# Token chunks of two fused feed-forward layers: six pairs of 512 to 488 columns in place of five of 512 and one of 448

## Chip, cores and metric

The kernel runs on one core of a Trainium2 chip. The metric is the device time of one execution in microseconds (us), from three executions of the kernel before: 1044.4, 1044.48 and 1044.66, so the median is 1044.48 us.

## What is computed

The input is a matrix v of 256 channels by N = 6016 tokens. An attention over channels mixes its rows, and two feed-forward layers of inner width 2048 follow, all in 32-bit floating point.

```python
qn = q / (np.linalg.norm(q, axis=1, keepdims=True) + 1e-06)
kn = k / (np.linalg.norm(k, axis=1, keepdims=True) + 1e-06)
s = kn.transpose(0, 2, 1) @ qn / tau          # 256 x 256
a = softmax(s, axis=-1)
x = (v @ a).reshape(6016, 256)
h = x @ w_in;  x = (h / (1 + np.exp(-1.702 * h))) @ w_out           # layer 0
h = x @ w_in2; x = (np.maximum(h, 0) + alpha * np.minimum(h, 0)) @ w_out2   # layer 1
```

## The kernel before, in words

A first stage (about 52 us) computes the 256 x 256 matrix of scores, its softmax, and folds it into the first layer's inner weights. What is left is two layers over the tokens, and these take nearly all the time.

**Tiling.** The tokens stand along the free axis, cut into 12 chunks whose widths are the list WIDTHS (L28). Two neighbouring chunks make a pair, so there are six pairs per layer, numbered 0 to 5. Within a pair both chunks have the same width n. Each layer's 2048 inner units are cut into eight groups (index j) of two blocks of 128.

**Precision.** Every operand is kept as a high and a low half of type fp32r. A product is three matmuls with 128 x 128 weights and n moving columns each (PASSES, L37): high by high, high weights by low data, and low weights by high data. Each matmul has its own weight load.

**A quartet** (L766 to L846) is the work of one j of one pair: four blocks of the hidden layer (two blocks of units by two chunks) from seven products instead of eight, after Strassen and Winograd. The operands T1 to T4 of the seven products are sums and differences of the pair's blocks of data (prepare, L527). That makes 7 x 3 = 21 inner matmuls (L651, into the PSUM tile ps_h). Between them stand the outer products of the quartet before (Outs.next, L666 to L683): eight of three matmuls each, 24 in all (L680, into ps_o). So TensorE issues 45 matmuls in a quartet, eight quartets in a pair, 360 in a pair. Pair 0 of layer 0 is computed without that trick (direct, L744) with 24 inner and 24 outer matmuls for each j, always 512 columns wide (T). Layer 0 has quartets for its pairs 1 to 5 and layer 1 for its pairs 0 to 5: eleven pairs of quartets.

**Other engines.** ScalarE copies some of the PSUM tiles to SBUF (L777), applies the activation (L722, L726) and makes the high half (L734, L736). VectorE adds the two parts of a block (L711), does the second step of layer 1's activation (L730) and makes the low half (L740, L742). Beside these it runs steps from a list in the background: operands of the next pair (L541 to L550) and conversions of weights. That list is a planner's: each step has a fixed cost (0.7 us and so on), and a step is taken where the cost fits into a fixed gap (FREE, L31). Neither depends on the width.

**Transfers.** The chunks of the next pair are loaded at the second quartet of a pair (load_tokens, L245, called at L959 and L960), on SyncE's queue. A pair's results are copied from PSUM at its end (evacuate, L687 to L696) and stored: in layer 0 to the buffer x1 in device memory, in layer 1 to the output. The buffer x1 has a separate tensor for each chunk, with rows of n elements.

**Memory.** All SBUF and PSUM tiles of tokens are 512 columns wide whatever n is, and only their first n columns are used. The operands T3, T4 and B22 of the even pairs of layer 1 come from a separate pool (xin2, L537); all others come from one ring of eleven tiles.

**Order.** The order of the instructions on every engine is written out by hand (manual_schedule) and does not depend on the widths.

```python
WIDTHS = [512] * 10 + [448] * 2                                    # L28
...
n = WIDTHS[c0]                                                     # L769
...
nc.tensor.matmul(ps[:, :n], WI[:, wq, a, blk], x[:, b, :n], ...)   # L651
...
nc.tensor.matmul(acc_ps[c][d][:, :n], WO[:, j, a, f, d * P:(d + 1) * P], (hi, lo)[b][:, :n], ...)   # L680
```

Of the kernel before, what the change touches and what calls it, by code (L numbers as in the profile page):

```python
# [24 lines left out]
SLOTS = 4  # L25
RAWS = 2

WIDTHS = [512] * 10 + [448] * 2  # L28
assert sum(WIDTHS) == N

FREE = ((0.7, 2.8, 1.7), (0.0, 0.8, 0.8))  # L31
# [24 lines left out]
def attention_then_two_ffns(ctx: ExitStack, tc: tile.TileContext, q, k, vT, tau, w1i, w1o, w2i, w2o, alpha, outT):  # L56
# [14 lines left out]
    nc = tc.nc  # L71
    starts = [sum(WIDTHS[:c]) for c in range(len(WIDTHS))]
    NP = len(WIDTHS) // 2

# [12 lines left out]
    WO = wto.tile([P, NQ, 2, 2, C], F32R, name="wo")  # L87
    x1 = [dram.tile([P, 2, w], F32, name=f"x1_{c}") for c, w in enumerate(WIDTHS)]
    w2i_d = [dram.tile([P, 2, 7, P], F32R, name=f"w2i_{j}") for j in range(NQ)]
# [155 lines left out]
    def load_tokens(l, c):  # L245
        n = WIDTHS[c]
        raws[l, c] = cv.tile([P, 2, T], F32, tag="xraw", name="xraw", bufs=2)
        src = x1[c][:] if l else vT[:, starts[c]:starts[c] + n].rearrange("(a p) n -> p a n", p=P)
        nc.sync.dma_start(raws[l, c][:, :, :n], src)

    with tc.manual_schedule():
# [275 lines left out]
        def prepare(l, p):  # L527

            n = WIDTHS[2 * p]
            r0, r1 = raws.pop((l, 2 * p)), raws.pop((l, 2 * p + 1))  # L530
# [513 lines left out]
```

## Time and profile before

| what | value |
|---|---|
| median of three executions | 1044.48 us |
| the profiled execution, its own time | 1045.86 us |
| its span, from the first to the last instruction | 1044.1 us |
| TensorE clock granted, mean | 1.000 |
| TensorE busy (matmuls) | 1034.2 us, 99% of the span, 4658 matmuls |
| TensorE weight loads busy | 865.6 us, 83% |
| VectorE busy | 815.0 us, 78% |
| ScalarE busy | 750.6 us, 72% |
| mean traffic with device memory | 74 GB/s |

Matmuls overlap: the next one starts before the one ahead of it has left the array. So the busy share of TensorE is no measure of its speed, and neither is the duration of one matmul. What counts is the distance from the start of one matmul to the start of the next, which the timeline and the lengths of stages give. Below it is called the pace.

### The profile page before, as it was taken

The page shows a single profiled execution, that of the slowest core. Times are in us where ns is not written, and L with a number is a line of the kernel's source. Part 1 is how long each engine was busy: PE and PEld are TensorE (multiplying, and loading weights), DVE is VectorE, ACT ScalarE, POOL GpSimd, SP SyncE. Part 2 cuts the span into 40 slices and gives each one's busy share as a digit, 9 for nine tenths or more (in the row PEclk, how much of TensorE's full clock was granted, in tenths as well). Part 3 has the DMA queues.
Part 4 walks back from the last instruction along what each step waited for, and adds up shares of the span by engine and source line. Part 5 has one row for each costly group of instructions (what it writes and reads, how often), then busy time and mean ns, then how long its engine had stood idle before and what let it go on. Part 6 is the DMA issues. An engine that isn't in the chain of part 4 may idle for free.

```text
span 1044.1 us, 12624 instructions
## 1 busy us (share of the span) xinstructions
PE 1034.2 (99%) x4658; PEld 865.6 (83%) x4658; DVE 815.0 (78%) x1318; ACT 750.6 (72%) x1255; POOL 32.6 (3%) x43
## 2 busy tenths in 40 slices
PE   8999999999999999999999999999999999999998
PEld 7788888888888888888998888888888888888897
DVE  5789978888788888555647888888888888888776
ACT  6677668777687777667767777777777777767775
POOL 4400000000000000000110000000000000000000
PEclk9999999999999999999999999999999999999999
DMA  9625203115225223003444002002001000100100
GB/s 359 235 75 174 74 11 106 61 56 177 76 81 177 76 96 131 1 1 122 161 167 152 1 1 82 1 1 81 1 1 47 35 1 21 57 1 1 41 1 35
DMA packets 30462, 77.63 MB, mean 74 GB/s; under 512 B 3008, under 2 KB 7616, under 8 KB 30144
## 3 DMA queue, kind: packets, MB, share of 16 engines
q1 hardware_dynamic: 28096, 65.29, 17.6%
q0 software_dynamic: 2304, 11.54, 3.3%
q8 instruction: 36, 0.59, 0.3%
q14 instruction: 26, 0.21, 0.1%
HBM read 52.96 MB, written 23.86 MB: 74 GB/s over the span
## 4 chain that ended last, share of the span: by engine, by line
PE 89%; DMA 4%; ACT 3%; DVE 3%; issue 1%; SPq 0%; ACTq 0%; DVEq 0%
PE ps_o L680 47%; PE ps_h L651 41%; DMA qk<-in_q 2%; ACT ghi L736 1%; PE pw L474 1%; ACT g L722 1%; DMA qs<-in_q 1%; DMA xraw<-in_vT 1%; DVE g L711 1%; DMA qk<-in_k 0%; ACT s L777 0%; DVE glo L742 0%; PE gram L337 0%; DVE ob L694 0%; DVE top L133 0%
## 5 line engine op out<-in xcount | busy, mean ns | idle before, releaser
L680 PE MATMUL ps_o<-ghi,wo 128*128 128x512 f32 (+1 forms) x1536 | 563.7, 386 | 0.0
L651 PE MATMUL ps_h<-x,wi 128*128 128x512 f32 (+1 forms) x2040 | 554.5, 387 | 1.0 <-ACT wi L482 0.7
L651 PEld LDWEIGHTS ps_h<-x,wi 128*128 128x128 f32 x2040 | 381.1, 188 | 78.4 <-ACT s L777 3.2
L680 PEld LDWEIGHTS ps_o<-ghi,wo 128*128 128x128 f32 x1536 | 288.3, 188 | 55.5
L680 PE MATMUL ps_o<-glo,wo 128*128 128x512 f32 (+1 forms) x768 | 296.2, 386 | 0.5 <-DVE glo L740 0.5
L711 DVE TENSOR_TENSOR g<-ps_h,s 128x512 f32<-128x512 f32 (+1 forms) x264 | 178.5, 676 | 92.5 <-PE ps_h L651 53.8
L777 ACT COPY s<-ps_h 128x512 f32<-128x512 f32 (+1 forms) x264 | 152.1, 576 | 91.3 <-PE ps_h L651 90.1
L734 ACT ACTIVATE ghi<-g,sign_sb 128x512 fp32r<-128x512 f32 (+1 forms) x192 | 136.8, 713 | 71.6 <-DVE g L730 70.1
L740 DVE SCALAR_TENSOR_TENSOR glo<-g,sign_sb,ghi 128x512 fp32r<-128x512 f32 (+1 forms) x192 | 141.3, 736 | 44.7 <-ACT ghi L734 38.4
L680 PEld LDWEIGHTS ps_o<-glo,wo 128*128 128x128 f32 x768 | 144.2, 188 | 28.5 <-DVE glo L740 0.8
L742 DVE TENSOR_TENSOR glo<-g,ghi 128x512 fp32r<-128x512 f32 (+1 forms) x192 | 126.0, 674 | 32.9 <-ACT ghi L736 32.9
L726 ACT ACTIVATE g<-g,sign_sb 128x512 f32<-128x512 f32 (+1 forms) x144 | 102.3, 711 | 28.2 <-DVE g L711 28.2
L730 DVE SCALAR_TENSOR_TENSOR g<-g,slope_sb 128x512 f32<-128x512 f32 (+1 forms) x144 | 105.8, 735 | 18.9 <-ACT g L726 18.8
L736 ACT CAST ghi<-g 128x512 fp32r<-128x512 f32 (+1 forms) x192 | 113.2, 611 | 3.6
L722 ACT ACTIVATE g<-g 128x512 f32<-128x512 f32 (+1 forms) x120 | 74.7, 623 | 38.0 <-DVE g L711 37.8
L722 ACT ACTIVATE g<-ps_h 128x512 f32<-128x512 f32 (+1 forms) x72 | 42.1, 585 | 10.4 <-PE ps_h L651 9.6
L337 PE MATMUL gram<-qk 128*128 128x256 f32 x156 | 33.9, 379 | 1.9 <-DMA qk<-in_k 1.9
L730 DVE SCALAR_TENSOR_TENSOR g<-ps_h,slope_sb,g 128x512 f32<-128x512 f32 (+1 forms) x48 | 35.0, 730 | 0.0
L337 PEld LDWEIGHTS gram<-qk 128*128 128x128 f32 x156 | 29.5, 190 | 6.2 <-issue 2.2
L726 ACT ACTIVATE g<-ps_h,sign_sb 128x512 f32<-128x512 f32 (+1 forms) x48 | 32.0, 667 | 1.0 <-ACT g L726 0.3
L542 ACT CAST x<-t 128x512 fp32r<-128x512 f32 (+1 forms) x44 | 26.8, 611 | 4.6 <-DVE t L550 4.6
L546 DVE TENSOR_TENSOR x<-t,x 128x512 fp32r<-128x512 f32 (+1 forms) x44 | 29.0, 671 | 0.0
(101 smaller groups left out, 476.5 us busy)
## 6 DMA issues: line engine op xcount, KB each, us to landing
wi<-w2i POOLq DMA_DIRECT2D x8, 896.0 KB, 4.9
xraw<-in_vT SPq DMA_DIRECT2D x10, 512.0 KB, 5.9
x<-ob SPq DMA_DIRECT2D x20, 256.0 KB, 2.4
xraw<-x SPq DMA_DIRECT2D x10, 512.0 KB, 5.6
out_T<-ob SPq DMA_DIRECT2D x20, 256.0 KB, 2.0
qk<-in_q SPq DMA_DIRECT2D x9, 512.0 KB, 10.2
qk<-in_k SPq DMA_DIRECT2D x9, 512.0 KB, 10.3
raw<-in_w2i SPq DMA_DIRECT2D x8, 512.0 KB, 4.1
```

The source lines that it names most:

```text
L337: nc.tensor.matmul(gram[m][:, :C], tiles[i][:, 1, r, m * P:(m + 1) * P], tiles[i][:, 0, r, :], start=(t == 0), stop=(t == R - 1))
L651: nc.tensor.matmul(ps[:, :n], WI[:, wq, a, blk], x[:, b, :n], start=(start and i == 0), stop=(stop and i == 2), skip_group_check=True)
L680: nc.tensor.matmul(acc_ps[c][d][:, :n], WO[:, j, a, f, d * P:(d + 1) * P], (hi, lo)[b][:, :n], start=(start and i == 0), stop=(stop and i ...
L711: nc.vector.tensor_tensor(self.src, ps[:, :self.n], s[:, :self.n], ALU.add)
L722: nc.scalar.activation(self.g, self.src, AF.Gelu_apprx_sigmoid)
L726: nc.scalar.activation(self.g, self.src, AF.Copy, scale=sign_sb[:, self.f])
L730: nc.vector.scalar_tensor_tensor(self.g, self.src, slope_sb[:, self.f], self.g, ALU.mult, ALU.max)
L734: nc.scalar.activation(self.hi, self.g, AF.Copy, scale=sign_sb[:, self.f])
L736: nc.scalar.copy(self.hi, self.g)
L740: nc.vector.scalar_tensor_tensor(self.lo, self.g, sign_sb[:, self.f], f32(self.hi), ALU.mult, ALU.subtract)
L742: nc.vector.tensor_tensor(self.lo, self.g, f32(self.hi), ALU.subtract)
L777: nc.scalar.copy(s[:, :n], ps[:, :n])
```

## The change

Each chunk of a pair keeps one width, but the six pairs are now 512, 508, 504, 500, 496 and 488 columns wide. The sum of the twelve widths stays 6016. Every slice and every address of a token follows from the list; nothing else is edited.

```diff
-WIDTHS = [512] * 10 + [448] * 2
+WIDTHS = [w for w in (512, 508, 504, 500, 496, 488) for _ in range(2)]
 assert sum(WIDTHS) == N
```

## Rows read from the trace of the kernel before

**Rows 1.** The page: busy time by engine, and the granted clock in 40 slices.
```profile
PE 1034.2 (99%) x4658; PEld 865.6 (83%) x4658; DVE 815.0 (78%) x1318; ACT 750.6 (72%) x1255; POOL 32.6 (3%) x43
...
PEclk9999999999999999999999999999999999999999
```

**Rows 2.** The page: the chain that ended last, shares of the span by engine.
```profile
PE 89%; DMA 4%; ACT 3%; DVE 3%; issue 1%; SPq 0%; ACTq 0%; DVEq 0%
```

**Rows 3.** Stages, one pair each: from:to, length, busy us and instructions by engine.
```profile
146.31:228.48 82.17, 82.10 (x361) 67.36 (x360) 68.66 (x134) 61.58 (x112) 0.00 (x0) 1.00 0.20 68
...
392.47:474.45 81.98, 81.91 (x362) 67.50 (x360) 51.13 (x85) 56.74 (x101) 0.00 (x0) 1.00 0.12 42
474.45:548.09 73.64, 73.64 (x362) 67.63 (x361) 41.37 (x70) 50.92 (x98) 7.04 (x13) 1.00 0.47 159
548.09:630.38 82.29, 82.29 (x362) 67.51 (x361) 66.84 (x100) 59.52 (x97) 1.60 (x3) 1.00 0.14 48
630.38:712.22 81.84, 81.84 (x361) 67.47 (x360) 68.69 (x102) 60.63 (x98) 0.00 (x0) 1.00 0.07 26
712.22:795.04 82.82, 82.82 (x361) 67.50 (x360) 68.71 (x102) 60.91 (x98) 0.00 (x0) 1.00 0.08 26
...
959.61:1040.35 80.74, 80.23 (x385) 71.70 (x383) 60.88 (x98) 56.62 (x96) 0.00 (x0) 1.00 0.04 16
```

**Rows 4.** Timeline of TensorE, layer 0, pair 3: start, length, instruction; same place, next quartets.
```profile
350.61 1.52 PE L651 MATMUL ps_h<-x,wi 128*128 128x512 f32 x6
...
360.81 1.52 PE L651 MATMUL ps_h<-x,wi 128*128 128x512 f32 x6
```

**Rows 5.** Timeline of TensorE, layer 0, pair 5: same place of two quartets.
```profile
501.88 1.38 PE L651 MATMUL ps_h<-x,wi 128*128 128x448 f32 x6
...
511.00 1.38 PE L651 MATMUL ps_h<-x,wi 128*128 128x448 f32 x6
```

**Rows 6.** Timeline of TensorE, layer 1, pair 5: same place of two quartets.
```profile
996.69 1.40 PE L651 MATMUL ps_h<-x,wi 128*128 128x448 f32 x6
...
1005.99 1.40 PE L651 MATMUL ps_h<-x,wi 128*128 128x448 f32 x6
```

**Rows 7.** Timeline of TensorE, layer 1, pair 0: products with T2, T3 and T4.
```profile
572.32 0.84 PE L651 MATMUL ps_h<-x,wi 128*128 128x512 f32 x3
...
574.36 0.86 PE L651 MATMUL ps_h<-x,wi 128*128 128x512 f32 x3
...
576.46 0.95 PE L651 MATMUL ps_h<-x,wi 128*128 128x512 f32 x3
```

**Rows 8.** Timeline of TensorE: back-to-back matmuls of 256 columns, first and last.
```profile
67.14 0.40 PE L474 MATMUL pw<-wi_hi,eT_lo 128*128 128x256 f32 x2
...
67.85 0.40 PE L474 MATMUL pw<-wi_hi,eT_lo 128*128 128x256 f32 x2
```

**Rows 9.** Groups by line and shape, weight loads: busy us, mean ns, idle before.
```profile
L651 PEld LDWEIGHTS ps_h<-x,wi 128*128 128x128 f32 x2040 | 381.1, 188 | 78.4 <-ACT s L777 3.2 <-ACT wi L482 1.2 <-DVE wi L486 0.5
```

**Rows 10.** Groups by line and shape, VectorE: busy us, mean ns, idle before.
```profile
L711 DVE TENSOR_TENSOR g<-ps_h,s 128x512 f32<-128x512 f32 x216 | 148.6, 688 | 60.0 <-PE ps_h L651 37.7 <-ACT s L777 16.3 <-issue 0.6
...
L711 DVE TENSOR_TENSOR g<-ps_h,s 128x448 f32<-128x448 f32 x48 | 29.9, 624 | 32.6 <-PE ps_h L651 16.1 <-ACT s L777 15.1 <-issue 0.6
```

**Rows 11.** Waits: who waited for whom, us in total, times, longest us.
```profile
PEld ps_h L651 <- ACT s L777: 3.2, 9, 0.5
```

**Rows 12.** Transfers by issue: count, KB each, median us to landing.
```profile
xraw<-x SPq DMA_DIRECT2D x10, 512.0 KB, 5.6
...
xraw<-x SPq DMA_DIRECT2D x2, 448.0 KB, 4.4
```

**Rows 13.** Timeline, the end: last store issued and last copy.
```profile
1039.06 2.26 SPq L696 DMA_DIRECT2D out_T<-ob  x4
...
1040.34 0.62 DVE L694 COPY ob<-ps_o 128x448 f32<-128x448 f32 x1 [0.59 <-PE ps_o L680]
```

## The prediction, made before the changed kernel was run

> **What bounds the kernel now.** I read the page's first two parts first. TensorE is busy for 99% of the span and holds the full clock, the 2.4 GHz level, in all 40 slices [rows 1]. VectorE comes next at 78%. The chain that ended last lies on TensorE for 89% of the span [rows 2], and what is left of it is mostly the start. So the time is the number of matmuls times their pace, the distance from one start to the next.
>
> The stages give the pace. A pair is 360 matmuls [rows 3]. Pairs of 512 columns in layer 0 take 81.98 to 82.17 us (two of the four such pairs are shown), that is 227.7 to 228.3 ns a matmul, a few stalls included. Pair 5 with 448 columns takes 73.64 us, 204.6 ns. The timeline shows the pace without stalls, from the same place in two neighbouring quartets of 45 matmuls:
> - 512 columns: 10.20 us [rows 4], 226.7 ns each. The columns alone take 512/2.4 = 213.3 ns, so 13.3 ns are on top.
> - 448 columns, layer 0: 9.12 us [rows 5], 202.7 ns. The columns take 186.7 ns, 16.0 ns on top.
> - 448 columns, layer 1: 9.30 us [rows 6], 206.7 ns, 20.0 ns on top.
>
> So what stands on top of the columns is not one constant. The same 512 columns show it as well: in an even pair of layer 1, nine matmuls take 2.04 us up to the product with T3 and 2.10 us from there [rows 7], which is 226.7 and then 233.3 ns. There 13.3 ns have become 20.0 ns. These slow stretches make the even pairs of layer 1 last 82.29 and 82.82 us against 81.84 us for an odd one [rows 3].
>
> I read this so: 13.3 ns is the best case, which 512 columns settle into when nothing disturbs them, and 16 to 20 ns is what a matmul pays when it isn't settled. The profile does not say what decides that.
>
> **The change part by part.** No instruction is added, removed or moved, since the order and the planner's costs don't depend on widths. In each layer the columns before are 5 x 512 + 448 = 3008, after 512 + 508 + 504 + 500 + 496 + 488 = 3008. Anything that costs a fixed time plus a time for each column comes out the same.
>
> VectorE is such a thing: 688 ns at 512 columns, 624 at 448 [rows 10], 1 ns a column. ScalarE is treated alike. At the narrowest width VectorE's 102 instructions of a pair lose about 24 ns each, so its 68.69 us [rows 3] become some 66.2 us beside about 79 us of matmuls. It stays covered, and I put it at 0. The stalls behind ScalarE's copies sum to 3.2 us in nine waits [rows 11]. A copy shrinks with its chunk and so does the cover. I take 0, with 1 us either way.
>
> Transfers: a chunk lands 5.6 us after issue (512 KB) or 4.4 us (448 KB) [rows 12]. It is issued in the second quartet and used from the third on, about 10 us later. Rows of 508 columns are no longer a power of two long, and no row shows what that costs. Below nothing would be a faster landing, which no one waits for; above, a landing 5 us later still comes in time. I put it at 0.
>
> The end: the last chunk grows by 40 columns, from 448 to 488. The last copy of 0.62 us [rows 13] grows by 0.04 us, the two or three VectorE steps that TensorE waits for at the end by as much each, the last store hardly. I take +0.2 us.
>
> So everything hangs on the pace at 508, 504, 500, 496 and 488 columns, which no row shows. It is used by 5 pairs x 360 = 1800 matmuls in each layer. The bounds come from the rows: 13.3 ns on top, as at an undisturbed 512, and 20.0 ns, as at 448 in layer 1. I take 16.0 ns, the value of [rows 5]. That row is the nearest in kind: a width other than 512, from the ring of tiles that nearly all these products use, in a stage without stalls. By it the five paces are 227.7, 226.0, 224.3, 222.7 and 219.3 ns, together 1120.0 ns.
> - Layer 0: before, 4 x 226.7 + 202.7 = 1109.3 ns. The difference of 10.7 ns times 360 is +3.8 us.
> - Layer 1: before, 4 x 226.7 + 206.7 = 1113.3 ns, and +6.7 ns times 360 is +2.4 us. But pairs 2 and 4 already pay about 3 ns a matmul over the settled pace (82.82 us against 81.84 us). I count those extras once, which takes off 2 x 360 x 2.7 ns = 1.9 us. This leaves +0.5 us.
>
> The sum is 3.8 + 0.5 + 0.2 = +4.5 us. The profiled execution took 1045.86 us with a span of 1044.1 us, and would become 1050.4 us. The median shown is 1.4 us lower, 1044.48 us, and gives 1049.0 us.
>
> A second reading leads close to the same place: the pace may move in steps. 226.7 to 233.3 ns and 200 to 206.7 ns are each 6.7 ns, which is 16 columns at 2.4 GHz. If a part of 16 columns costs as much as a whole one, 508, 504 and 500 cost what 512 does, and 496 and 488 cost 220.0 ns. That gives 1120.0 ns again, +3.8 and +2.4 us without the deduction, and 1050.9 us with the end. Both readings are in the forecast.
>
> **The rivals.** *Faster: 448 is the odd width out.* A floor lies under the pace at 448, and all the new widths stand above it, at n/2.4 + 13.3 ns. Its place is the pair of 448 columns in each layer, and it decides if the floor is under 216.7 ns, the pace of 488 columns. Its price: layer 0 loses 2.7 ns x 360 = 1.0 us, layer 1 6.7 x 360 = 2.4 us, less the 0.2 us at the end: 3.2 us, 1041.3 us. For it speaks the weight load: 188 ns [rows 9] plus a hand-over of some 15 to 19 ns would be 203 to 207 ns, just the two paces at 448. Against it, matmuls of 256 columns follow each other in (67.85 - 67.14)/6 = 0.118 us [rows 8], each with a load of its own. So a load need not cost 188 ns of pace. And the two paces at one width are not what a floor gives.
>
> The Trainium skill, TensorE: Matmul & The Clock Gate, section LDWEIGHTS (loading the stationary operand), puts a load of 128 columns at 128/1.2 = 107 ns. The 118 ns fit that, and by it there is no floor at 448.
>
> *No change.* If the pace is a straight line between the two widths in each layer, equal columns give an equal time, 1044.7 us with the end. For it speaks that only two widths were measured. Against it, that line rises by (226.7 - 202.7)/64 = 0.375 ns or 0.31 ns a column, slower than the 0.417 ns that a column takes, so something else would have to shrink with width.
>
> The Trainium skill, the same page, section Back-to-back issue gap, gives N/2.4 + 2.5 ns for an isolated gap at full clock. That is a straight line, and with equal columns the sum would be 0. The trace has 226.7 ns where it gives 215.8, and 202.7 and 206.7 where it gives 189.2.
>
> *Much slower: nothing settles.* All five widths pay 20.0 ns on top, as in [rows 6] and in the slow stretch of [rows 7]. Layer 0: 360 x (1140.0 - 1109.3) ns = +11.0 us. Layer 1: 360 x 26.7 ns = +9.6 us, less the 1.9 us which pairs 2 and 4 pay now. With the end +18.9 us, 1063.4 us. For it speaks that the 448-column pair of layer 1 stays at 206.7 ns for quartet after quartet; against it, that layer 0 does not.
>
> **How the numbers follow.** I give the forecast, either reading, 0.46, the faster rival 0.26, no change 0.12, much slower 0.16. A measurement of this kernel can tell about 0.2%, 2.1 us, from no change. The forecast is at +4.5 to +6.4 us, and with 1 us for the stalls it lies outside of that but for a mixture, in which some widths settle and some do not. From it I give 0.02 to no change. The faster rival is at -3.2 us, with stalls -2 to -4, all but faster; half a settled case would fall within. Faster 0.26, within 0.2% 0.14, slower 0.60. The range has to take in both signs. It goes from 1041.0 us, which holds most of the faster rival, to 1060.0 us, which holds the lower half of the much slower one. The forecast's own range is 1047 to 1053 us.
>
> **What would show it.** In the changed kernel the same place of two quartets tells the pace of each width: 45 times the pace, so 10.25 us at 508 columns for the forecast, 10.13 if settled, 10.43 if not at all; at 488 columns 9.87, 9.75 and 10.05 us. Pair 5 of layer 0 should last about 79.0 us and pairs 1 to 4 within 1 us of today's. The pair of 512 columns in layer 1 should keep its time. VectorE's busy time should not move by over 2 us, nor its share in any pair pass 90%. The prediction is wrong if the narrower pairs run at n/2.4 + 13.3 ns, or if TensorE shows idle time that it doesn't show now, before a product or behind a late chunk.

## The result, and the profile after

The changed kernel takes 1056.36 us (median of five executions, 1055.87 to 1056.85), against 1044.66 us for the kernel before in the same session. The ratio is 1.0112 with an interval of 1.0099 to 1.0125, so it is slower by 11.7 us. The profiled execution took 1056.56 us with a span of 1054.8 us, 10.7 us longer than before.

The page of the changed kernel: busy time by engine, the granted clock in 40 slices, and the chain that ended last by engine.

```profile
PE 1045.8 (99%) x4658; PEld 868.4 (82%) x4658; DVE 815.6 (77%) x1318; ACT 752.5 (71%) x1255; POOL 32.6 (3%) x43
...
PEclk9999999999999999999999999999999999999999
...
PE 91%; DMA 3%; DVE 2%; ACT 2%; SPq 1%; issue 0%; ACTq 0%; DVEq 0%
```

Beside [rows 1, 2] nothing has changed its kind. The instructions are as many, the clock stands at the 2.4 GHz level in every slice, VectorE and ScalarE moved by 0.6 and 1.9 us, and TensorE's share of the chain rose from 89% to 91%. What grew is TensorE's own time, by 11.6 us. The stages say where.

Stages of the changed kernel, pairs 1 to 5 of layer 0 and then 0 to 5 of layer 1, with the columns of [rows 3].

```profile
146.42:228.83 82.41, 82.34 (x361) 67.42 (x360) 68.41 (x134) 61.38 (x112) 0.00 (x0) 1.00 0.20 68
228.83:310.78 81.95, 81.93 (x362) 67.55 (x360) 66.69 (x116) 61.26 (x112) 0.00 (x0) 1.00 0.33 112
310.78:392.51 81.73, 81.72 (x361) 67.68 (x360) 68.48 (x125) 61.40 (x112) 0.00 (x0) 1.00 0.32 111
392.51:473.27 80.76, 80.71 (x362) 67.67 (x360) 50.78 (x85) 55.66 (x101) 0.00 (x0) 1.00 0.13 44
473.27:554.38 81.11, 81.11 (x362) 68.06 (x361) 43.46 (x70) 53.94 (x98) 7.04 (x13) 1.00 0.42 144
554.38:637.20 82.82, 82.82 (x362) 67.58 (x360) 67.04 (x100) 59.79 (x97) 1.59 (x3) 1.00 0.15 49
637.20:719.36 82.16, 82.16 (x361) 67.58 (x360) 68.30 (x102) 60.63 (x98) 0.00 (x0) 1.00 0.08 26
719.36:801.32 81.96, 81.96 (x361) 67.63 (x360) 67.89 (x102) 60.39 (x98) 0.00 (x0) 1.00 0.08 26
801.32:882.74 81.42, 81.42 (x362) 67.61 (x360) 67.46 (x102) 60.05 (x98) 0.00 (x0) 1.00 0.08 26
882.74:963.47 80.73, 80.73 (x362) 67.65 (x360) 66.97 (x102) 59.59 (x98) 0.00 (x0) 1.00 0.07 26
963.47:1051.00 87.53, 86.92 (x385) 72.31 (x383) 64.69 (x98) 60.27 (x96) 0.00 (x0) 1.00 0.04 15
```

- The pair that went from 448 to 488 columns costs +7.5 us in layer 0 (81.11 against 73.64 us) and +6.8 us in layer 1 (87.53 against 80.74 us).
- The four pairs that lost 4 to 16 columns give nearly nothing back. In layer 0 they differ by +0.2, 0.0, -0.3 and -1.2 us, in layer 1 by +0.3, -0.9, -0.4 and -2.0 us.
- Pair 0 of layer 1, still 512 wide, takes +0.5 us. Its first quartet carries the last 24 outer products of layer 0, which are now 488 columns wide: 24 times some 23 ns is 0.5 us. This belongs to layer 0.

Together that is +6.7 us for layer 0 and +3.8 us for layer 1, 10.5 of the 10.7 us of the span. The timeline shows why. Each two lines below are the same place of two neighbouring quartets, and the distance of their starts over 45 is the pace.

Timeline of TensorE in the changed kernel, layer 0, pairs 1 to 5.

```profile
187.18 1.53 PE L651 MATMUL ps_h<-x,wi 128*128 128x508 f32 x6
...
197.43 1.52 PE L651 MATMUL ps_h<-x,wi 128*128 128x508 f32 x6
...
269.30 1.52 PE L651 MATMUL ps_h<-x,wi 128*128 128x504 f32 x6
...
279.50 1.52 PE L651 MATMUL ps_h<-x,wi 128*128 128x504 f32 x6
...
350.76 1.52 PE L651 MATMUL ps_h<-x,wi 128*128 128x500 f32 x6
...
360.96 1.52 PE L651 MATMUL ps_h<-x,wi 128*128 128x500 f32 x6
...
422.35 1.51 PE L651 MATMUL ps_h<-x,wi 128*128 128x496 f32 x6
...
432.40 1.50 PE L651 MATMUL ps_h<-x,wi 128*128 128x496 f32 x6
...
502.93 1.52 PE L651 MATMUL ps_h<-x,wi 128*128 128x488 f32 x6
...
513.07 1.52 PE L651 MATMUL ps_h<-x,wi 128*128 128x488 f32 x6
```

| columns | forecast pace, ns | layer 0: quartet us, pace ns, over n/2.4 | layer 1: quartet us, pace ns |
|---|---|---|---|
| 508 | 227.7 | 10.25, 227.8, 16.1 | 10.25, 227.8 |
| 504 | 226.0 | 10.20, 226.7, 16.7 | 10.24, 227.6 |
| 500 | 224.3 | 10.20, 226.7, 18.3 | 10.20, 226.7 |
| 496 | 222.7 | 10.05, 223.3, 16.7 | 10.08, 224.0 |
| 488 | 219.3 | 10.14, 225.3, 22.0 | 10.17, 226.0 |

504 and 500 columns run at exactly the pace that 512 had in [rows 4], 226.7 ns. 488 columns are slower than 496. At 488 columns neighbouring quartets differ by 0.03 us; on average they take 10.16 us, 225.7 ns, in both layers.

The covered work stayed covered. The waits of the changed kernel show the stalls behind ScalarE's copies at 3.0 us in nine waits, against 3.2 us [rows 11].

```profile
PEld ps_h L651 <- ACT s L777: 3.0, 9, 0.5
```

Its transfers by issue show rows of 508 columns landing after 5.7 us, against 5.6 us for 512 [rows 12], and 488 after 4.5 us. VectorE's steps on 488 columns take 666 ns, between the 624 ns of 448 and the 688 ns of 512 [rows 10].

### The profile page after: what moved, and what is told of

It is laid out like the page before. It is cut to its first block, busy times and chain, and to the rows that moved or that the text cites. A ratio compares the mean times of both kernels' runs of the same rounds, so it can differ in the third digit from the quotient of the medians.

```text
span 1054.8 us, 12624 instructions
## 1 busy us (share of the span) xinstructions
PE 1045.8 (99%) x4658; PEld 868.4 (82%) x4658; DVE 815.6 (77%) x1318; ACT 752.5 (71%) x1255; POOL 32.6 (3%) x43
## 4 chain that ended last, share of the span: by engine, by line
PE 91%; DMA 3%; DVE 2%; ACT 2%; SPq 1%; issue 0%; ACTq 0%; DVEq 0%
PE ps_o L680 48%; PE ps_h L651 42%; DMA qk<-in_q 2%; PE pw L474 1%; DMA qs<-in_q 1%; DMA xraw<-in_vT 1%; ACT ghi L736 1%; ACT g L722 0%; SPq L358 0%; DVE g L711 0%; PE gram L337 0%; DVE glo L742 0%; ACT s L777 0%; DVE ob L694 0%; ACT wi L482 0%
## 5 line engine op out<-in xcount | busy, mean ns | idle before, releaser
L680 PE MATMUL ps_o<-ghi,wo 128*128 128x512 f32 (+5 forms) x1536 | 567.9, 389 | 0.0
L651 PE MATMUL ps_h<-x,wi 128*128 128x512 f32 (+5 forms) x2040 | 559.1, 390 | 0.8 <-ACT wi L482 0.7
L651 PEld LDWEIGHTS ps_h<-x,wi 128*128 128x128 f32 x2040 | 382.0, 188 | 81.6 <-ACT s L777 3.0
L680 PEld LDWEIGHTS ps_o<-ghi,wo 128*128 128x128 f32 x1536 | 289.1, 188 | 58.7
L680 PE MATMUL ps_o<-glo,wo 128*128 128x512 f32 (+5 forms) x768 | 298.8, 389 | 0.4 <-DVE glo L740 0.4
L711 DVE TENSOR_TENSOR g<-ps_h,s 128x508 f32<-128x508 f32 (+5 forms) x264 | 178.8, 677 | 101.6 <-PE ps_h L651 58.9
L777 ACT COPY s<-ps_h 128x508 f32<-128x508 f32 (+5 forms) x264 | 152.0, 576 | 100.4 <-PE ps_h L651 99.0
L734 ACT ACTIVATE ghi<-g,sign_sb 128x512 fp32r<-128x512 f32 (+5 forms) x192 | 136.8, 712 | 70.3 <-DVE g L730 68.9
L740 DVE SCALAR_TENSOR_TENSOR glo<-g,sign_sb,ghi 128x512 fp32r<-128x512 f32 (+5 forms) x192 | 141.5, 737 | 44.8 <-ACT ghi L734 38.5
L680 PEld LDWEIGHTS ps_o<-glo,wo 128*128 128x128 f32 x768 | 144.5, 188 | 30.3 <-DVE glo L740 0.9
L742 DVE TENSOR_TENSOR glo<-g,ghi 128x512 fp32r<-128x512 f32 (+5 forms) x192 | 126.2, 675 | 32.9 <-ACT ghi L736 32.9
L730 DVE SCALAR_TENSOR_TENSOR g<-g,slope_sb 128x512 f32<-128x512 f32 (+5 forms) x144 | 105.9, 736 | 18.9 <-ACT g L726 18.9
L736 ACT CAST ghi<-g 128x512 fp32r<-128x512 f32 (+5 forms) x192 | 113.1, 610 | 3.6
```

Source lines behind the costliest of these rows:

```text
L711: nc.vector.tensor_tensor(self.src, ps[:, :self.n], s[:, :self.n], ALU.add)
L730: nc.vector.scalar_tensor_tensor(self.g, self.src, slope_sb[:, self.f], self.g, ALU.mult, ALU.max)
L734: nc.scalar.activation(self.hi, self.g, AF.Copy, scale=sign_sb[:, self.f])
L736: nc.scalar.copy(self.hi, self.g)
L740: nc.vector.scalar_tensor_tensor(self.lo, self.g, sign_sb[:, self.f], f32(self.hi), ALU.mult, ALU.subtract)
L742: nc.vector.tensor_tensor(self.lo, self.g, f32(self.hi), ALU.subtract)
```

## The experiments

So nearly all of the 11.7 us is a matter of pace. Three questions followed. Is the pace TensorE's own (A), or do other engines that use the memories disturb it (B)? Does it depend on the width only, or on where data and weights lie against each other (R), or on the place in PSUM (P)? And does it depend on what ran before (H)? Kernels are compared with the kernel before, and the edits are against it, unless said otherwise. "Bare" kernels compute none of the reference: they are rows of matmuls by 128 x 128 weights of type fp32r, each with its own weight load, with TensorE alone at work.

**e1: the widths by themselves.** 96 matmuls for each setting, the twelve weight blocks and six data blocks in turn, starting `at` columns into a block (`wat` for weights).

```diff
+for i in range(count):
+    w = W[:, (i % 12) * P + wat:(i % 12) * P + wat + P]
+    x = X[:, (i % 6) * T + at:(i % 6) * T + at + n]
+    nc.tensor.matmul(banks[i // 3 % 4][:, :n], w, x, start=(i % 3 == 0), stop=(i % 3 == 2))
```

> This kernel computes none of the reference: it issues 96 matmuls each, every one with its own weight load, at 20 widths from 512 down to 256 columns, and then at a few shifted addresses, with no other engine at work beside them; its output is a constant. Theory A (TensorE's own pace at odd widths is slow): the paces of the changed kernel come back without any other engine: 226.7 ns at 512 and 504, 223 to 227 at 500 and 496, 225 to 228 at 508 and 488, 203 to 207 at 448, and 512 columns that start 16 columns off are slower than 226.7 by 6 ns or more. Theory B (other engines or transfers slow the matmuls): every width comes out on the line n/2.4 + 13.3 ns, so 216.7 at 488 and 200.0 at 448, wherever the columns start.

Stages of the bare kernel, in order: 512, 508, 504, 488, 448 and 384 columns, then 512 columns with the data starting 16 columns later, with the weights 16 later, and with both 16 later. Columns: from:to, length, busy us and count of matmuls, of weight loads, of ScalarE and of GpSimd, clock, share of DMA, GB/s.

```profile
34.06:55.82 21.76, 21.76 (x98) 18.03 (x96) 0.00 (x0) 0.00 (x0) 1.00 0.00 0
55.82:77.67 21.85, 21.85 (x97) 18.03 (x96) 0.00 (x0) 0.00 (x0) 1.00 0.00 1
77.67:99.43 21.76, 21.76 (x97) 18.02 (x96) 0.00 (x0) 0.00 (x0) 1.00 0.00 1
...
163.65:184.76 21.11, 21.11 (x97) 18.02 (x96) 0.00 (x0) 0.00 (x0) 1.00 0.00 1
...
307.61:327.06 19.45, 19.45 (x97) 18.03 (x96) 0.00 (x0) 0.00 (x0) 1.00 0.00 1
...
383.14:399.82 16.68, 16.68 (x98) 16.68 (x98) 0.00 (x0) 0.00 (x0) 1.00 0.00 1
470.05:492.03 21.98, 21.98 (x97) 18.03 (x96) 0.00 (x0) 0.00 (x0) 1.00 0.00 1
559.12:581.51 22.39, 22.39 (x97) 18.06 (x96) 0.00 (x0) 0.00 (x0) 1.00 0.00 1
603.83:625.61 21.78, 21.78 (x97) 18.02 (x96) 0.00 (x0) 0.00 (x0) 1.00 0.00 0
```

Length over 96 is the pace: 226.7 ns at 512, 227.6 at 508, 226.7 at 504, 202.6 at 448, the full kernel's values at these widths to 0.2 ns. No other engine is needed for them, so A holds. 384 columns take 173.7 ns, 256 columns 120.0 ns, each 13.3 to 13.7 ns over its columns. A floor under the pace of 448 would have held these up, so there is none. The last three lines were the surprise. Data shifted by 16 columns cost 2 ns a matmul (expected were 6 or more), weights shifted by 16 cost 6.6 ns, and both shifted by 16 cost nothing. What counts is how the two lie against each other. Two values did not fit: 500 and 488 columns took 223.3 and 219.9 ns here, and 226.7 and 225.3 in the changed kernel.

**e2: steps of 16 columns in the full kernel.** It leaves out the last 512 tokens.

```diff
-WIDTHS = [512] * 10 + [448] * 2
-assert sum(WIDTHS) == N
+WIDTHS = [w for w in (512, 480, 464, 448, 432, 416) for _ in range(2)]
+assert sum(WIDTHS) <= N
```

> Widths 512, 480, 464, 448, 432, 416 in the whole kernel; the last 512 tokens are left out, so the total time (some 960 us) is not to be compared, only the pace of each pair. Theory A with steps of 16 columns: multiples of 16 run at n/2.4 + 13.3 ns: 213.3 at 480, 206.7 at 464, 200.0 at 448, 193.3, 186.7. Theory A with steps of 32 columns: 480 and 416 (multiples of 32) at 213.3 and 186.7, but 464 and 432 like the next multiple of 32, 213.3 and 200.0. Theory C (only 512 settles): 16 to 20 ns over the columns at all of them, 216 to 220 at 480. 448 in second-to-third place of the list also tells if its two paces (202.7 and 206.7) go with the width or with the place.

480 columns took 216.7 ns, 464 took 209.9, 432 about 196 and 416 about 188, 15 to 17 ns over their columns. None came down to 13.3 ns, though all are multiples of 16, so both forms of theory A with steps fall. And 448 took both of its paces in one execution, with the layers exchanged. Timeline, pair 3 of layer 0, then of layer 1:

```profile
338.38 1.40 PE L651 MATMUL ps_h<-x,wi 128*128 128x448 f32 x6
...
347.68 1.40 PE L651 MATMUL ps_h<-x,wi 128*128 128x448 f32 x6
...
797.75 1.38 PE L651 MATMUL ps_h<-x,wi 128*128 128x448 f32 x6
...
806.87 1.38 PE L651 MATMUL ps_h<-x,wi 128*128 128x448 f32 x6
```

9.30 us is 206.7 ns, 9.12 us is 202.7 ns; in [rows 5, 6] the slow one stood in layer 1. So neither the layer nor the width decides. In layer 0 the pace changed within the pair: in its seventh quartet a weight load waited 0.5 us for a copy of ScalarE, and the eighth took 9.12 us.

**e3: the separate pool moved by 64 bytes.** In the addresses of the built program the ring's tiles, the activated blocks that L680 streams and the weights start at 128 modulo 256 bytes, the pool of T3, T4 and B22 at 192. A larger pad beside the pool puts it at 128.

```diff
-pad = ...tile([P, 8], F32, name="pad")
+pad = ...tile([P, 24], F32, name="pad")
```

> The widths of before; the small tile ahead of the separate operand pool is 96 bytes instead of 32, which moves that pool's three tiles by 64 bytes, so that they start at the same place within 128 bytes as the ring's tiles. Theory A (pace depends on where a stream of columns starts and ends): the slow stretches of the even pairs of layer 1 go, these pairs last 81.8 us like the odd ones, and the time falls by about 0.5 + 1.0 + 0.9 = 2.4 us to 1042.1. Theory B (the slow stretches come from other work in those pairs): nothing moves, 1044.6 us.

1041.45 us, ratio 0.9966 (0.9954 to 0.9979), some 3 us quicker than before. Stages of pairs 0, 2 and 4 of layer 1:

```profile
548.40:629.71 81.31, 81.31 (x361) 67.51 (x360) 66.83 (x100) 59.39 (x96) 1.60 (x3) 1.00 0.14 49
711.54:793.34 81.80, 81.80 (x361) 67.49 (x360) 68.72 (x102) 60.74 (x97) 0.00 (x0) 1.00 0.08 26
875.17:956.87 81.70, 81.70 (x361) 67.48 (x360) 68.02 (x102) 60.53 (x98) 0.00 (x0) 1.00 0.07 25
```

The slow stretches of [rows 7] are gone: 82.29, 82.82 and 82.72 us became 81.31, 81.80 and 81.70. Pair 5 of layer 1, whose operands did not move, now ran at 202.7 ns, against 206.7 before [rows 6].

**e4: what ran before.** Bare again: 36 matmuls of one width, then 72 of another, on the same tiles. Other entries shift the data, the weights or the place in PSUM. The edit is against e1. An entry names the columns, the shift of the data, the shift of the weights, the distance between data blocks (`pitch`), the start in PSUM (`out`), whether a pause comes first, and the number of matmuls.

```diff
-run(n, at, count, wat)
+run(n, at, wat, pitch, out, pause, count)
...
+[508, 0, 0, 512, 0, 0, 36], [488, 0, 0, 512, 0, 0, 72], [504, 0, 0, 512, 0, 0, 36], [488, 0, 0, 512, 0, 0, 72],
```

> None of the reference is computed; bare matmuls, each with its own weight load, no other engine beside them but for some pauses. First part: 488, 500, 496 and 448 columns, 36 matmuls each, entered from eight other widths and after a pause. Theory H (one width has more than one pace and keeps the one that it fell into): at least at one of these widths two steady paces appear, 220.0 and 225.7 ns at 488 or 202.7 and 206.7 ns at 448 or 223.3 and 226.7 at 500, by what ran before. Theory W (in the kernel something else slows 488 to 225.7): bare matmuls of 488 columns run at 220.0 whatever ran before, of 448 at 202.7. Second part: 512 columns with data or weights shifted by 64 to 256 columns, and 448 with data shifted, with another start in the PSUM bank and with other distances between the streams. Theory R (weight load and data stream meet in SBUF, by the place of one against the other): shifts of the data slow 512 to 229 to 234 ns until the shift is a multiple of some larger block, and some shift at 448 gives 200.0 ns; the start in PSUM changes nothing. Rival P (it is the writing into PSUM): the start in PSUM changes the pace.

Stages of 72 matmuls, columns as in e1: 488 after 512, 488 after 504; 448 after 512, 448 after 508; 512 with data 64 later; 448 with data 16 later; 448 with the PSUM start 16 later.

```profile
37.33:53.57 16.24, 16.24 (x74) 13.62 (x72) 0.00 (x0) 0.00 (x0) 1.00 0.00 0
86.22:102.06 15.84, 15.84 (x74) 13.52 (x72) 0.00 (x0) 0.00 (x0) 1.00 0.01 1
...
723.12:737.72 14.60, 14.60 (x74) 13.54 (x73) 0.00 (x0) 0.00 (x0) 1.00 0.00 1
745.91:760.78 14.87, 14.87 (x73) 13.52 (x72) 0.00 (x0) 0.00 (x0) 1.00 0.00 1
938.39:954.71 16.32, 16.32 (x73) 13.52 (x72) 0.00 (x0) 0.00 (x0) 1.00 0.00 1
1049.42:1063.82 14.40, 14.40 (x73) 13.51 (x72) 0.00 (x0) 0.00 (x0) 1.00 0.00 1
1093.10:1107.69 14.59, 14.59 (x74) 13.53 (x72) 0.00 (x0) 0.00 (x0) 1.00 0.00 1
```

The same instructions on the same addresses take 225.6 or 220.0 ns at 488 columns and 202.8 or 206.5 at 448, by what ran before, and keep it (H); a pause ahead of the 72 did not free 488 columns from the 225.6 ns. A shift of the data by 64 columns, 256 bytes, costs nothing (226.7 ns), one of 16 brings 448 to 200.0 ns, 13.3 over its columns. The place in PSUM does nothing (202.6 ns): P falls. In this second part each entry also follows another one, so a single shifted value can owe something to what ran before it; the 226.7 ns of 512 columns came back whenever data and weights lay against each other as at the start.

**e5: 488 as the second pair.** 488 here follows a 512-wide pair in both layers.

```diff
+WIDTHS = [w for w in (512, 488, 508, 504, 500, 496) for _ in range(2)]
```

> The changed kernel with 488 columns in pair 1 and 508 to 496 in pairs 2 to 5. If 225.7 ns belong to 488 columns in this kernel, pair 1 of layer 0 lasts about 81.3 to 81.6 us and the time stays at 1056. If they belong to the last place (or to what ran ahead of it), pair 1 runs at 220.0 ns, 79.2 us, pair 5 with 496 columns at 223.3 ns, and the time falls by 5.7 ns x 720 = 4.1 us to 1052.

1055.64 us, 1.0105 (1.0089 to 1.0122). In layer 0 the stage of 488 columns took 80.11 us, with 9.90 us a quartet (220.0 ns) from its third on, in layer 1 81.40 us, and there it stood at 10.15 us a quartet, 225.6 ns. Both paces came in one execution, so both expectations were half right; the order of the pairs is worth under 1 us.

**e6: two pairs of 480, four of 512.**

```diff
+WIDTHS = [w for w in (512, 512, 512, 512, 480, 480) for _ in range(2)]
```

> Widths 512 four times and 480 twice. By the bare pace of 480 columns, 216.7 ns, layer 0 needs (3 x 226.7 + 2 x 216.7) x 360 ns = 400.8 us for pairs 1 to 5 against 399.4 before, and layer 1 as much as before: +1.4 us, 1046 us. If the sum of columns decided, 1044.7. If the kernel's 480 columns ran as badly above the bare pace as 488 do (5.7 ns), +8 us more, 1054.

1046.96 us, 1.0022 (1.0013 to 1.0032), 1 us from the expected 1046. One quartet of 480 took 9.75 us, 216.7 ns, as in e1 and e2. With a width whose pace is known the sum comes out.

**e7: the pad of e3, and 448 columns stored 16 columns later** (the matmul in e4 that took 200.0 ns). AT is used for the operands of L651 and L680 and where they are written.

```diff
+AT = {448: 16}
+def cols(n):
+    return slice(AT.get(n, 0), AT.get(n, 0) + n)
...
-x[:, b, :n]
+x[:, b, cols(n)]
```

> The widths of before, the small tile of 96 bytes as in e3, and in the 448-column chunks the operands lie in columns 16 to 463 of their tiles instead of 0 to 447. Theory R (what counts is where the data stream lies against the weights): the 448-column pairs run at 200.0 ns as the bare matmuls did with that shift, 45 x 200 = 9.00 us a quartet against 9.12 us, so 1.0 us less in each layer than in e3: 1041.45 - 1.9 = 1039.5 us. Rival (the bare result does not carry over, since the pace in the kernel hangs on its history): 202.7 or 206.7 ns as before, 1041.5 us or 1 to 2 us more.

1040.07 us, 0.9960 (0.9946 to 0.9973). A quartet of 448 took 9.00 us, 200.0 ns, as in e4.

**e8: seven widths, each at 16 starts** of 0 to 60 columns; bare, 42 matmuls each, entries as in e4.

```diff
+[508, 0, 0, 576, 0, 0, 42], [508, 4, 0, 576, 0, 0, 42], [508, 8, 0, 576, 0, 0, 42],
```

> None of the reference is computed: bare matmuls of 508, 504, 500, 496, 488, 480 and 448 columns, the data shifted by 0 to 60 columns in steps of 4, 42 matmuls each. Theory R: each width has its own good and bad shifts; for multiples of 16 (496, 480, 448) at least one shift gives n/2.4 + 13.3 ns, that is 220.0, 213.3 and 200.0. If the width alone set the pace, every shift of one width would give the same, 223.3 at 496, 216.7 at 480. Open, and the question for the changed kernel: whether 508, 504, 500 and 488, which are no multiples of 16, reach that line at any shift (225.0, 223.3, 221.7 and 216.7 ns) or stay 2 ns or more above it, which would make them bad widths wherever they lie.

The pace is that of the last 24 matmuls of each entry.

| columns | 508 | 504 | 500 | 496 | 488 | 480 | 448 |
|---|---|---|---|---|---|---|---|
| quickest pace, ns | 226.7 | 226.7 | 220.0 | 220.0 | 220.0 | 213.3 | 200.0 |
| slowest pace, ns | 233.3 | 233.3 | 229 | 226.8 | 226.7 | 220.0 | 206.7 |

The three values that theory R asked for at 496, 480 and 448 came. Every quickest pace is a multiple of 6.67 ns, 16 columns at 2.4 GHz. Between 512 and 504 columns there is nothing to win, and 488 to 500 share one pace at best. Stages of 500 columns at start 0 and at start 4, 42 matmuls each:

```profile
328.08:337.61 9.53, 9.53 (x44) 7.90 (x43) 0.00 (x0) 0.00 (x0) 1.00 0.00 0
337.61:346.86 9.25, 9.25 (x43) 7.88 (x42) 0.00 (x0) 0.00 (x0) 1.00 0.00 0
```

226.9 against 220.2 ns: four columns further on, the same work is 3% quicker. Start 0 had given 500 columns 223.3 ns in e1, so here too what ran before can count as well as the start; e10 and e11 try the start in the full kernel.

**e9: the changed kernel with the pad of e3.**

```diff
-WIDTHS = [512] * 10 + [448] * 2
+WIDTHS = [w for w in (512, 508, 504, 500, 496, 488) for _ in range(2)]
...
-pad = ...tile([P, 8], F32, name="pad")
+pad = ...tile([P, 24], F32, name="pad")
```

> The changed kernel with the small tile of 96 bytes, as in e3. Theory R: only the even pairs of layer 1 move: pair 0 from 82.8 to 81.8 us, pair 2 (504) from 227.7 to 226.7 ns, pair 4 (496) from 224.2 to 223.3 ns, some 1.0 + 0.4 + 0.3 us, so 1054.7 us. If the widths cost 11.7 us because of the pool's place, the time returns to about 1045.

1050.2 us, 1.0063 (1.0047 to 1.0078), 4.5 us better than expected. Its four executions took 1049.88, 1050.17, 1050.24 and 1053.19 us; the first was traced, so what the last one did differently isn't known. Pairs 3, 4 and 5 of layer 0, in which TensorE reads nothing from the moved pool, got quicker too: 81.05, 79.86 and 79.36 us against 81.73, 80.76 and 81.11. Timeline of pair 5, layer 0 and then layer 1:

```profile
500.63 1.48 PE L651 MATMUL ps_h<-x,wi 128*128 128x488 f32 x6
...
510.53 1.48 PE L651 MATMUL ps_h<-x,wi 128*128 128x488 f32 x6
...
1006.75 1.52 PE L651 MATMUL ps_h<-x,wi 128*128 128x488 f32 x6
...
1016.92 1.52 PE L651 MATMUL ps_h<-x,wi 128*128 128x488 f32 x6
```

9.90 us is the 220.0 ns of the bare run, 10.17 us the 226.0 ns of the changed kernel. Both stand in one trace with the same instructions.

**e10: e9 with starts from e8**, used as in e7.

```diff
+AT = {508: 4, 500: 4, 496: 12, 488: 20}
```

> The changed kernel as in e9, and the operands of each width lie where its bare matmuls were quick: 508 and 500 columns start at column 4 of their tiles, 496 at 12, 488 at 20, 504 at 0. No width, no column and no instruction is changed. Theory R (the loss is the place of the data stream against the weights): paces of 226.7, 226.7, 220.0, 220.0 and 220.0 ns, against 227.5, 226.7, 226.7, 223.3 and 225.7 in the changed kernel; that is 360 x (0.8 + 0 + 6.7 + 3.3 + 5.7) = 5.9 us less in each layer and some 1043 us in all, 12 us below e9. Rival (the widths themselves are bad in the kernel, wherever they lie): no more than 1 us below e9.

1049.72 us, 1.0050 (1.0036 to 1.0064), a miss: only 0.5 us below e9. By that number the rival holds, but not by its reason, since 508 columns took 226.7 ns and 500 settled at 220.0. 496 reached 220.0 only into its second quartet and then stayed at 224.0 in layer 0 and 226.7 in layer 1, and 488 took 223.3 in both layers. A start that was quickest in the bare run is not stable against the full kernel's interruptions.

**e11: the stable ones alone.** The pad, four pairs of 500 that start 4 columns in, one of 496 that starts 12 in.

```diff
+WIDTHS = [w for w in (512, 500, 500, 500, 500, 496) for _ in range(2)]
+AT = {500: 4, 496: 12}
```

> Widths 512, four times 500 and 496, with the tile of 96 bytes and starts at column 4 for 500 and 12 for 496. The bare matmuls ran at 220.0 ns for both. Theory R: five pairs at 220.0 ns are 1100.0 ns a layer, against 4 x 226.7 + 200.0 = 1106.7 in e7, so 2.4 us less a layer: 1040.1 - 4.8 = 1035.3 us. If a width that is no multiple of 16 falls back to a worse pace in the kernel (226.7 at 500, as in the changed kernel), 226.7 x 4 + 223.3 = 1130.0 ns, 1057 us.

1038.47 us, 0.9939 (0.9926 to 0.9953): the quickest version here, some 6 us below the kernel before and 18 below the changed one, with the same columns. It stayed 3.2 us above the expected 1035.3. 500 columns held 9.90 us a quartet, 220.0 ns, in all eight pairs; 496 lost it in layer 1 (224.0 ns, some 1.4 us of the 3.2).

**e12: the changed kernel with the two engines of the copies at a pair's end exchanged** (L694), which alters only how a pair is entered. The edit is against the changed kernel.

```diff
-(nc.scalar.copy if d == 0 else nc.vector.tensor_copy)(ob[:, :n], acc_ps[c][d][:, :n])
+(nc.scalar.copy if d == 1 else nc.vector.tensor_copy)(ob[:, :n], acc_ps[c][d][:, :n])
```

> The changed kernel, with ScalarE and VectorE exchanged in the two copies of a finished chunk at a pair's end; no tile, address, width or matmul differs, only the moment at which a few waits at the border of two pairs end. In e9 pairs 3 to 5 of layer 0 took other paces (pair 5 at 220.0 ns) although none of their operands had moved. Theory H (a width keeps the pace that it falls into at such a border): at least one pair of 500, 496 or 488 columns takes another of the paces seen for its width, and the time leaves 1056.4 us by 1 us or more, to between 1048 and 1058. Rival (in e9 it was the move of the tiles behind the pool, which hold copies and results): all paces stay, 1056.4 us.

1055.23 us, 1.0098 (1.0081 to 1.0115), 1.1 us less than the changed kernel. The two intervals overlap, but its executions, 1054.68 to 1055.71 us, all lie below the changed kernel's. Pair 3, of 500 columns, took 10.05 us a quartet instead of 10.20 (223.3 against 226.7 ns) in most quartets of both layers, and its stages lasted 81.05 and 80.74 us, 0.7 us less each. The 488 columns stayed at 10.14 us. The entry has an effect, but a small one, and it did not bring back the 220.0 ns of e9. For pair 3 of layer 0 it gives e9's 81.05 us without moving a tile; for pairs 4 and 5 it stays open whether e9's gain came from the entry or from the moved tiles that hold copies and results.

## Why the prediction was right in direction and wrong in size

- **The bound, the cover and the end held.** TensorE's pace decides. Transfers, VectorE and the stalls were costed at nothing, and their own time did not change: the stalls sum to 3.0 us against 3.2 us. From the start of the last copy to the end of the span it is 3.9 us, against 3.8 us.
- **The step that failed is "I take 16.0 ns", one value on top of the columns for all five widths**, carried over from the only other width in the trace. The runs show 16.1, 16.7, 18.3, 16.7 and 22.0 ns, and the last lies above the 20.0 ns that the prediction took as its bound: a quartet of 488 columns took 10.14 us where it had 9.75 to 10.05. In layer 0 the paces sum to 1129.8 ns instead of 1120.0, which is 9.8 x 360 = 3.5 us; in layer 1 to 1132.1 ns, 4.4 us more. With them the terms of +3.8 and +0.5 us become +7.3 and +4.9 us, where the stages show +6.7 and +3.8, since not every quartet of a pair ran at the pace of the table. Of the 9.8 ns, 488 columns make 6.0 and 500 make 2.3. At 508 columns the term was exact.
- **The reading behind it failed too**: 13.3 ns when nothing disturbs the matmuls, 16 to 20 when they aren't settled. In e1 nothing else runs, and 448 and 508 columns still pay 16.0 ns, while 500 columns come down to 11.7 ns (220.0 ns, e8 and e11).
- **"The profile does not say what decides that" overlooked what the trace of the kernel before shows.** Timeline of TensorE, layer 1, pair 5, 448 columns:

```profile
970.65 0.77 PE L651 MATMUL ps_h<-x,wi 128*128 128x448 f32 x3
...
973.08 0.77 PE L651 MATMUL ps_h<-x,wi 128*128 128x448 f32 x3
...
974.90 0.50 PEld L651 LDWEIGHTS ps_h<-x,wi 128*128 128x128 f32 x3 [0.21 <-ACT s L777]
...
976.85 0.78 PE L651 MATMUL ps_h<-x,wi 128*128 128x448 f32 x3
...
979.95 0.78 PE L651 MATMUL ps_h<-x,wi 128*128 128x448 f32 x3
```

Twelve matmuls take 2.43 us ahead of one wait of 0.21 us for a copy of ScalarE, 202.5 ns each, and fifteen take 3.10 us behind it, 206.7 ns, which then holds to the end of the pair. So the 20.0 ns of [rows 6] set in at a single stall. In the changed kernel pair 3 of layer 1 went from 223.4 to 226.7 ns at a wait of 0.27 us. The stalls were put at nothing, yet the pace of what follows can change with them. This is read from the moment of the change, here and in e2 and e10 (waits of 0.5 us); it was not tested by itself. Nor does every stall do it: a wait of 0.2 us in the same pair of e3 left 202.7 ns as it was.

- **The deduction for pairs 2 and 4 of layer 1 held.** These two stages, 82.82 and 82.72 us before, lost 0.9 and 2.0 us though their paces came out at 227.6 and 224.0 ns, so what they had paid over the settled pace was not paid twice.
- **The second reading, steps of 16 columns, was nearer to the truth than the first**: 508, 504 and 500 did cost what 512 does, to 1.1 ns. It gave 220.0 ns for 496 and 488, which both reach in bare runs (e4, e8) and in pairs of e9, but not in the changed kernel. And 500 columns can reach 220.0 ns as well, which rounding up to parts of 16 columns does not give.
- **The rivals.** The floor falls by 384 columns at 13.7 ns on top in e1. The straight line falls, since all five narrower widths stand above it in both layers. "Nothing settles" was nearest for 488 columns alone, at 22.0 ns against its 20.0. The sum of the faster rival left out the 1.9 us that pairs 2 and 4 of layer 1 would have given back by its own condition.

What is shown: slow paces at these widths come up with TensorE alone; the pace depends on how data and weights lie against each other, up to 6.7 ns for the same work; and one set of instructions can have two or more paces, of which it keeps one for many matmuls. That the weight load and the data stream get in each other's way as they read SBUF is inferred from the shifts. Matmuls without their weight loads were not tried. What stays open is which pace a pair takes on entry or behind a stall: the bare runs gave 488 columns 220.0 ns after 496, and the changed kernel, where they follow 496 as well, gave them 225.3. Nor is a stall the only moment. In pair 3 of layer 0 of the changed kernel and in pair 4 of layer 1 of e10 the pace rose with no wait of TensorE in the trace, while the DMA engines were 96% and 99% busy; whether the transfers had a part in it was not tested.

## What to carry to other kernels

A width that the trace does not hold has no price until its pace is measured, at the place in memory that it will have: 4 columns fewer may bring nothing, and 24 fewer may cost more than 16 fewer. Read the pace from the same place of two neighbouring rounds, in every stage, look for a width that has two, and then for the matmul at which one pace gives way to the other. For 512 columns, put the data tiles and the weight tiles at the same offset modulo 256 bytes. For narrower chunks measure the start as well, since the quickest lay elsewhere (16 columns on at 448, 4 at 500), and choose widths that hold their pace through the kernel's own interruptions (500 columns here) rather than those that were quickest alone.

## What the runs showed of the hardware that was not expected

- Shifting the data or the weights by 4 to 32 columns makes 512-column matmuls 2 to 7 ns slower (228.9 to 233.3 ns), shifting both by 16, or either of them by 64, does not (226.7 ns).
- The Trainium skill, TensorE: Matmul & The Clock Gate, section Step-by-step: what each phase is for, says that loading the next weights takes no SBUF read bandwidth from the running matmul. If it is these two reads that meet, as inferred above, the runs speak against that for fp32r matmuls: the weights' address alone moves the pace from 226.7 to 233.3 ns.
- A pace can hold for a whole pair and be another one in the next layer: 448 columns at 202.7 and 206.7 ns, 488 at 220.0 and 225.6 ns. A single stall of 0.2 to 0.5 us can be where it changes. The quickest paces of e8 are all multiples of 6.67 ns; 500 columns at 220.0 ns pay 11.7 ns over their columns, less than the 13.3 ns of 512.
